# Converting float64 weights on chip: the high mantissa masked into 8 to 9, two additions to VectorE's share, GpSimd's share taken away

## The chip, the cores and the metric

The kernel runs on one core of a Trainium2 chip. The metric is the device time of one execution in microseconds (us). Of the kernel before there are three timed runs and one profiled execution, whose trace gives every instruction's start and duration.

## The reference

An mLSTM cell with 4 batches, 8 heads, 768 positions and 40 features per head is followed by a feed-forward block. Per head and position:

```
m_new  = max(f + m, i);  f_stab = exp(f + m - m_new);  i_stab = exp(i - m_new)
C = f_stab * C + i_stab * (v outer k);   n = f_stab * n + i_stab * k
y = sigmoid(o) * (C q) / max(|n . q|, 1)
x = y as (3072, 320)
h = x @ w_in          # (320, 2048)
out = (h - tanh(h)) @ w_out    # (2048, 320)
```

The two weight matrices arrive as float64. They are sent to the chip as 64-bit integers, and the kernel makes float32 of them.

## The kernel before

The sequence is cut into units of 128 positions of one batch, 24 in all. For each unit the cell part loads q, k, v, the output gate and a row `E` of gate products; VectorE scans `E` (line 363, 128x1024); TensorE makes the scores `ps`, which VectorE multiplies into `E` (line 394); TensorE makes `ph` from `E`, from the carried `state` and from `qg`, and `pc`, the new part of the state, which VectorE adds (lines 434 and 436); VectorE divides and gates (lines 416 to 421, the last writes `ys`), and TensorE transposes `ys` into `px`, which ScalarE copies to `xT`. GpSimd prepares `vs` (line 376), `qg` (line 379) and the decayed `state` (line 383) in `prepare`.

Two units make a group of 256 tokens. For a group and a pair of feature blocks, `up` makes `ph_up` from `xT` and `w_in` (12 matmuls as the profile counts them), ScalarE squares it twice (`z`, `q`, lines 500 and 501), VectorE makes `gt` of that (lines 502 and 503), and `down`, two items later, multiplies `gt` by `w_out` into `po`. Where the pairs of a group are done in more than one run, `po` is evicted into `part` (line 521 on VectorE, 523 on ScalarE); `po` has one buffer per token tile, so the next accumulation waits for the eviction.

The order on TensorE is written out by hand: `keep` chains every matmul to the one before. `STAGES` lists which pairs of which groups are taken in which order while the cell is still at work, and `merge` mixes the pieces of cell, feed-forward and conversion by their costs. On the other engines the framework's scheduler sets the order within what the data allow, and each engine then works through its own queue in that order.

The weights are 40 blocks: for each of the 8 pairs three of `w_in` (two of 128x256, one of 64x256) and two of `w_out` (128x320). A block is converted in three parts, a step apart from one another, so that the magnitude comes two steps after the fetch, and the sign two after that (`convert`, line 313; `weights`, line 273):

- fetch: the 64-bit words go to the staging tile `w64` (shown as `w`), eight buffers, from SP's queue (line 283);
- magnitude: VectorE masks the exponent out of the high word into `w_e` (295) and shifts the high word's mantissa up into `w_m` (298); ScalarE turns the exponent into the float's power of two (296), the shifted mantissa into a float of 1 to 2 (299) and the low word into a float `w_r` (300); GpSimd adds the two (301) and multiplies by the power of two (302);
- sign: VectorE takes the sign from the high word and sets it on `w_r` into `w_in` or `w_out` (306).

TensorE needs a pair's weights for the first time early in the cell part, so the conversion is spread over the same stretch as the cell and the first feed-forward items.

Of the kernel before, what the change touches and what calls it, by code (L numbers as in the profile page):

```python
# [34 lines left out]
FP = mybir.dt.float32  # L35
BF = mybir.dt.bfloat16
I32 = mybir.dt.int32
I64 = mybir.dt.int64
U32 = mybir.dt.uint32
AF = mybir.ActivationFunctionType  # L40
OP = mybir.AluOpType
# [20 lines left out]
def kernel(  # L62
# [14 lines left out]
    V, A, G = nc.vector, nc.scalar, nc.gpsimd  # L77
# [54 lines left out]
    conv = ctx.enter_context(tc.tile_pool(name="conv", bufs=2))  # L132
# [85 lines left out]
    for w in (after, ones):  # L218
        p = ps_b.tile([w.shape[1], NT, BH], FP, name="psum_lf", tag="b")
# [12 lines left out]
    xr, n, f = (mlp.tile([L, 2, NR], FP, name=name, tag=tag) for name, tag in (("xr", "z"), ("n", "z"), ("f", "q")))  # L232
# [40 lines left out]
    def weights(dst, src):  # L273

        p, n = dst.shape
        w = {}

        def fetch():
            if src.dtype == FP:
                nc.sync.dma_start(out=dst, in_=src)  # L280
                return
            w["st"] = conv.tile([128, n], I64, name="w64", tag="w64", bufs=8)[0:p]
            nc.sync.dma_start(out=w["st"], in_=src)

        def magnitude():
            if src.dtype == FP:
                return
            hi = w["hi"] = w["st"].bitcast(I32).rearrange("p (n two) -> p n two", two=2)[:, :, 1]
            lo = w["st"].bitcast(U32).rearrange("p (n two) -> p n two", two=2)[:, :, 0]
            e = conv.tile([128, n], I32, name="w_e", tag="w_e")[0:p]  # L290
            m = conv.tile([128, n], I32, name="w_m", tag="w_m")[0:p]
            r = w["r"] = conv.tile([128, n], I32, name="w_r", tag="w_r", bufs=4)[0:p]
            mf, rf = m.bitcast(FP), r.bitcast(FP)

            V.tensor_single_scalar(e, hi, 0x7FF00000, op=OP.bitwise_and)  # L295
            A.activation(out=e, in_=e, func=AF.Relu, scale=8.0, bias=rebias[0:p])  # L296

            V.tensor_single_scalar(m, hi, 12, op=OP.logical_shift_left)
            A.activation(out=mf, in_=m.bitcast(U32), func=AF.Copy, scale=2.0 ** -32, bias=1.0)  # L299
            A.activation(out=rf, in_=lo, func=AF.Copy, scale=2.0 ** -52)  # L300
            G.tensor_tensor(out=rf, in0=rf, in1=mf, op=OP.add)  # L301
            G.tensor_tensor(out=rf, in0=rf, in1=e.bitcast(FP), op=OP.mult)  # L302

        def sign():
            if src.dtype != FP:
                V.scalar_tensor_tensor(out=dst.bitcast(I32), in0=w["hi"], scalar=-(1 << 31), in1=w["r"],  # L306
                                       op0=OP.bitwise_and, op1=OP.bitwise_or)

        return fetch, magnitude, sign

    WB = 2 * 128

    def convert():

        blocks = []
        for p in range(NP):
            cols = slice(p * WB, (p + 1) * WB)
            for c, (r0, rows) in enumerate(KC):
                blocks.append(weights(w_in[0:rows, c, cols], moe_w_in[r0:r0 + rows, cols]))
            for f in (2 * p, 2 * p + 1):  # L320
                blocks.append(weights(w_out[:, f, :], moe_w_out[f * 128:(f + 1) * 128, :]))
        steps = []
        for x in range(len(blocks) + 4):
            def step(x=x):
                for late, part in enumerate((0, None, 1, None, 2)):
                    if part is not None and 0 <= x - late < len(blocks):
                        blocks[x - late][part]()
            steps.append((1.0, step))
        return steps
# [381 lines left out]
```

## Time and profile before

| | us |
|---|---|
| three runs, median (lowest, highest) | 682.23 (682.13, 682.42) |
| the profiled execution, whole | 682.25 |
| its span, first to last instruction | 680.5 |
| TensorE busy (matmul) | 612.6 |
| VectorE busy | 361.4 |
| ScalarE busy | 222.3 |
| GpSimd busy | 157.9 |

Engines are named PE (TensorE matmul), PEld (its weight load), DVE (VectorE), ACT (ScalarE), POOL (GpSimd) and SP (the queue that starts most transfers). A row of a group reads: line, engine, operation, out<-in, shape, count, then busy us and mean ns of one, then the engine's idle time just before these instructions and what ended most of it. A row of the timeline reads: start, duration, engine, line, operation, and in brackets the idle time before it and what ended it. Rows that follow one another closely are merged, with their count. The span between the starts of two successive operations can be shorter than a duration, since they overlap a little.

### The profile page before, as it was taken

The page shows a single profiled execution, that of the slowest core. Times are in us where ns is not written, and L with a number is a line of the kernel's source. Part 1 is how long each engine was busy: PE and PEld are TensorE (multiplying, and loading weights), DVE is VectorE, ACT ScalarE, POOL GpSimd, SP SyncE. Part 2 cuts the span into 40 slices and gives each one's busy share as a digit, 9 for nine tenths or more (in the row PEclk, how much of TensorE's full clock was granted, in tenths as well). Part 3 has the DMA queues.
Part 4 walks back from the last instruction along what each step waited for, and adds up shares of the span by engine and source line. Part 5 has one row for each costly group of instructions (what it writes and reads, how often), then busy time and mean ns, then how long its engine had stood idle before and what let it go on. Part 6 is the DMA issues. An engine that isn't in the chain of part 4 may idle for free.

```text
span 680.5 us, 8577 instructions
## 1 busy us (share of the span) xinstructions
PE 612.6 (90%) x3100; PEld 509.7 (75%) x3100; DVE 361.4 (53%) x617; ACT 222.3 (33%) x511; POOL 157.9 (23%) x170
## 2 busy tenths in 40 slices
PE   1469779787779999999999999999999999999996
PEld 1368657665667888888888888888888888878784
DVE  8686778977776336655553543553353333332321
ACT  2313545434632222322223322333233232242321
POOL 7534648645642010220220120111011000000000
PEclk9775979789979999999999999999999999999999
DMA  5637726346212011222221221221010000000000
GB/s 164 185 93 202 227 66 177 104 153 195 93 35 89 1 39 51 91 85 83 89 90 33 76 89 48 91 79 60 31 61 29 1 1 19 1 20 0 21 0 25
DMA packets 46210, 50.97 MB, mean 75 GB/s; under 512 B 3984, under 2 KB 38416, under 8 KB 46160
## 3 DMA queue, kind: packets, MB, share of 16 engines
q1 hardware_dynamic: 42288, 46.22, 22.5%
q10 hardware_dynamic: 3872, 4.13, 1.8%
q8 instruction: 26, 0.43, 0.2%
q14 instruction: 24, 0.20, 0.1%
HBM read 46.20 MB, written 4.13 MB: 74 GB/s over the span
## 4 chain that ended last, share of the span: by engine, by line
PE 78%; DVE 11%; issue 3%; POOL 3%; DMA 2%; ACT 2%; SPq 1%; ACTq 0%; DVEq 0%; POOLq 0%
PE ph_up L92 34%; PE po L92 28%; PE ps L92 6%; PE ph L92 6%; DVE E L363 2%; PE pc L92 2%; POOL w_r L301 2%; POOL w_r L302 1%; DMA E<-f_rows 1%; PE px L96 1%; DVE w_out L306 1%; DVE gt L503 1%; DVE gt L502 1%; DVE w_in L306 1%; DVE w_e L295 1%
## 5 line engine op out<-in xcount | busy, mean ns | idle before, releaser
L92 PE MATMUL ph_up<-xT,w_in 128*128 128x256 f32 x1152 | 318.9, 396 | 9.7 <-DVE gt L502 4.7
L92 PE MATMUL po<-w_out,gt 128*128 128x320 f32 x768 | 252.4, 442 | 3.9 <-DVE part L521 3.9
L92 PEld LDWEIGHTS ph_up<-xT,w_in 128*128 128x128 f32 x1152 | 203.1, 195 | 37.6 <-DVE gt L502 5.2
L502 DVE SCALAR_TENSOR_TENSOR gt<-ph_up,z 128x512 f32<-128x512 f32 x96 | 66.0, 689 | 208.5 <-ACT z L500 208.4
L92 PEld LDWEIGHTS po<-w_out,gt 128*128 128x128 f32 x768 | 132.7, 192 | 33.2 <-DVE part L521 4.9
L500 ACT ACTIVATE z<-ph_up 128x512 f32<-128x512 f32 x96 | 57.2, 595 | 253.7 <-PE ph_up L92 253.6
L92 PEld LDWEIGHTS ps<-q,kz 128*128 128x128 f32 x384 | 74.6, 218 | 21.2 <-DVE E L394 8.9
L92 PE MATMUL ps<-q,kz 128*128 128x128 f32 x384 | 80.2, 308 | 8.6 <-DVE E L394 8.6
L92 PEld LDWEIGHTS ph<-vs,E 128*128 128x128 f32 x384 | 71.7, 208 | 10.2 <-issue 0.5
L503 DVE SCALAR_TENSOR_TENSOR gt<-q,gt 128x512 f32<-128x512 f32 x96 | 70.6, 736 | 7.5 <-ACT q L501 1.4
L501 ACT ACTIVATE q<-z,tiny 128x512 f32<-128x512 f32 x96 | 69.1, 721 | 2.8
L92 PE MATMUL ph<-vs,E 128*128 128x41 f32 x384 | 61.9, 260 | 0.0
L363 DVE TENSOR_TENSOR_SCAN E<-E,diag 128x1024 f32<-128x1024 f32 x24 | 56.0, 2338 | 10.2 <-DMA E<-f_rows 10.2
L376 POOL TENSOR_TENSOR vs<-v,ei 128x640 f32<-128x640 f32 (+1 forms) x24 | 28.5, 1188 | 127.6 <-PE ph L92 123.0
L383 POOL TENSOR_TENSOR state<-state,eT 80x328 f32<-80x328 f32 x16 | 11.7, 734 | 163.7 <-DVE state L434 117.2
L394 DVE TENSOR_TENSOR E<-ps,E 128x512 f32<-128x512 f32 x48 | 32.9, 687 | 29.4 <-PE ps L92 29.0
L301 POOL TENSOR_TENSOR w_r<-w_r,w_m 128x256 f32<-128x256 f32 (+2 forms) x40 | 33.3, 834 | 58.6 <-ACT w_m L299 45.5
L92 PEld LDWEIGHTS pc<-vs,k 128*80 128x80 f32 x160 | 23.1, 170 | 21.8 <-issue 11.3
L379 POOL TENSOR_TENSOR qg<-qg,q 80x512 f32<-80x512 f32 x20 | 35.9, 1794 | 10.0 <-DMA qg<-g_rows 6.1
L92 PEld LDWEIGHTS ph<-state,qg 128*128 128x128 f32 x160 | 30.5, 197 | 9.7 <-issue 1.1
L92 PE MATMUL pc<-vs,k 128*80 128x82 f32 x160 | 25.3, 260 | 13.4 <-DVE ys L421 7.9
L296 ACT ACTIVATE w_e<-w_e,rebias 128x256 int32<-128x256 int32 (+2 forms) x40 | 21.0, 525 | 45.2 <-DVE w_e L295 45.1
(89 smaller groups left out, 368.9 us busy)
## 6 DMA issues: line engine op xcount, KB each, us to landing
E<-f_rows SPq DMA_DIRECT2D x24, 512.0 KB
w<-in_moe_w_out SPq DMA_DIRECT2D x16, 320.0 KB
w<-in_moe_w_in SPq DMA_DIRECT2D x16, 256.0 KB
kz<-in_kT SPq DMA_DIRECT2D x48, 80.0 KB
q<-in_qT SPq DMA_DIRECT2D x48, 80.0 KB
v<-in_v SPq DMA_DIRECT2D x24, 160.0 KB
k<-in_k SPq DMA_DIRECT2D x24, 160.0 KB
o<-in_o_gate SPq DMA_DIRECT2D x24, 160.0 KB
```

The costliest lines, as they stand in the source:

```text
L92: return cls.keep(nc.tensor.matmul(*args, **kwargs))
L296: A.activation(out=e, in_=e, func=AF.Relu, scale=8.0, bias=rebias[0:p])
L301: G.tensor_tensor(out=rf, in0=rf, in1=mf, op=OP.add)
L306: V.scalar_tensor_tensor(out=dst.bitcast(I32), in0=w["hi"], scalar=-(1 << 31), in1=w["r"], op0=OP.bitwise_and, op1=OP.bitwise_or)
L363: V.tensor_tensor_scan(out=row, data0=row, data1=diag.rearrange("p h t -> p (h t)"), initial=0.0, op0=OP.mult, op1=OP.add)
L376: G.tensor_tensor(out=t["vs"][:, both, :, 0:D], in0=t["v"].unsqueeze(1).to_broadcast(shape), in1=scale.unsqueeze(3).to_broadcast(shape), o ...
L379: G.tensor_tensor(out=t["qg"][0:TOP], in0=t["qg"][0:TOP], in1=t["q2"][0:TOP], op=OP.mult)
L394: V.tensor_tensor(out=P, in0=t["ps"], in1=P, op=OP.mult)
L500: A.activation(out=z, in_=ph, func=AF.Square, accum_out=sums[:, g * NP + p:g * NP + p + 1])
L501: A.activation(out=q, in_=z, func=AF.Square, bias=tiny)
L502: V.scalar_tensor_tensor(out=gt, in0=ph, scalar=TINY_POLY[0], in1=z, op0=OP.mult, op1=OP.mult)
L503: V.scalar_tensor_tensor(out=gt, in0=q, scalar=TINY_POLY[2], in1=gt, op0=OP.add, op1=OP.mult)
```

## The change

The magnitude's part is replaced by `split`, the sign's by `join`; the staging, the blocks and their steps stay.

- In `split` the two masks on VectorE stay, but the second now keeps the high word's 20 mantissa bits and sets the bits of 8.0 above them in the same instruction, which gives a float between 8 and 9. ScalarE makes the power of two and the low word's float as before; its conversion of the mantissa is gone.
- In `join` VectorE subtracts 7 and adds the low word's float, sets the sign on the power of two, and multiplies the two into the weight tile.
- GpSimd has no part in it any more.
- `w_e`, `w_m` and `w_r` have three buffers each; before, these were two, two and four.

```diff
-        def magnitude():
+        def split():
...
-            e = conv.tile([128, n], I32, name="w_e", tag="w_e")[0:p]
-            m = conv.tile([128, n], I32, name="w_m", tag="w_m")[0:p]
-            r = w["r"] = conv.tile([128, n], I32, name="w_r", tag="w_r", bufs=4)[0:p]
-            mf, rf = m.bitcast(FP), r.bitcast(FP)
+            e, m, r = (conv.tile([128, n], I32, name=name, tag=name, bufs=3)[0:p] for name in ("w_e", "w_m", "w_r"))
+            w["e"], w["m"], w["r"] = e, m, r
...
-            V.tensor_single_scalar(m, hi, 12, op=OP.logical_shift_left)
-            A.activation(out=mf, in_=m.bitcast(U32), func=AF.Copy, scale=2.0 ** -32, bias=1.0)
-            A.activation(out=rf, in_=lo, func=AF.Copy, scale=2.0 ** -52)
-            G.tensor_tensor(out=rf, in0=rf, in1=mf, op=OP.add)
-            G.tensor_tensor(out=rf, in0=rf, in1=e.bitcast(FP), op=OP.mult)
-
-        def sign():
-            if src.dtype != FP:
-                V.scalar_tensor_tensor(out=dst.bitcast(I32), in0=w["hi"], scalar=-(1 << 31), in1=w["r"],
-                                       op0=OP.bitwise_and, op1=OP.bitwise_or)
+            V.tensor_scalar(out=m, in0=hi, scalar1=0xFFFFF, scalar2=0x41000000, op0=OP.bitwise_and, op1=OP.bitwise_or)
+            A.activation(out=r.bitcast(FP), in_=lo, func=AF.Copy, scale=2.0 ** -52)
+
+        def join():
...
+            V.scalar_tensor_tensor(out=r, in0=m, scalar=-7.0, in1=r, op0=OP.add, op1=OP.add)
+            V.scalar_tensor_tensor(out=e, in0=w["hi"], scalar=-(1 << 31), in1=e, op0=OP.bitwise_and, op1=OP.bitwise_or)
+            V.tensor_tensor(out=dst, in0=r, in1=e.bitcast(FP), op=OP.mult)
```

One line fewer stands above them, so that after the change lines behind the conversion have a number lower by one (363 becomes 362, 502 becomes 501, 521 becomes 520); the masks are lines 293 and 296 now, the joining operations 304 to 306. The order on TensorE is the same, and GpSimd's is the same without its rows on `w_r`. VectorE's and ScalarE's orders are mixed anew.

The first place is VectorE's queue at the first eviction into `part` (tiles 208 and 209; the numbers behind `w_` are those of the staging tiles). Before, from the scan of `E` on:

```order
L363 SCALAR_TENSOR_TENSOR E<-E,diag 128x1024
L502 SCALAR_TENSOR_TENSOR gt<-ph_up,z 128x512
L503 SCALAR_TENSOR_TENSOR gt<-q,gt 128x512
L295 TENSOR_SCALAR w_e<-w_659 64x256
L298 TENSOR_SCALAR w_m<-w_659 64x256
L521 TENSOR_TENSOR part_208<-po,part_208 128x320
L521 TENSOR_TENSOR part_209<-po,part_209 128x320
```

Now, with 21 rows of conversion and one of `gt` between the same scan and the first of these:

```order
L293 TENSOR_SCALAR w_e<-w_743 64x256
L305 SCALAR_TENSOR_TENSOR w_e<-w_707,w_e 128x256
L501 SCALAR_TENSOR_TENSOR gt<-ph_up,z 128x512
L306 TENSOR_TENSOR w_in<-w_r,w_e 128x256
L502 SCALAR_TENSOR_TENSOR gt<-q,gt 128x512
L293 TENSOR_SCALAR w_e<-w_767 128x320
L296 TENSOR_SCALAR w_m<-w_767 128x320
L304 SCALAR_TENSOR_TENSOR w_r<-w_m,w_r 128x256
L305 SCALAR_TENSOR_TENSOR w_e<-w_721,w_e 128x256
L520 TENSOR_TENSOR part_208<-po,part_208 128x320
L306 TENSOR_TENSOR w_in<-w_r,w_e 128x256
L520 TENSOR_TENSOR part_209<-po,part_209 128x320
```

The eviction stood directly behind `gt` and two masks; now 28 rows of conversion in all, of seven blocks, lie between the scan and it.

The second place is VectorE's queue one scan earlier, at the gating of a unit (`ys_220`). Before:

```order
L306 SCALAR_TENSOR_TENSOR w_out<-w_500,w_r 128x320
L417 TENSOR_TENSOR den<-den,ph 128x8
L418 RECIPROCAL den<-den 128x8
L419 TENSOR_TENSOR o<-o,den 128x320
L421 TENSOR_TENSOR ys_220<-ph,o 128x320
L363 SCALAR_TENSOR_TENSOR E<-E,diag 128x1024
```

Now:

```order
L306 TENSOR_TENSOR w_in<-w_r,w_e 64x256
L416 TENSOR_TENSOR den<-den,ph 128x8
L304 SCALAR_TENSOR_TENSOR w_r<-w_m,w_r 128x320
L417 RECIPROCAL den<-den 128x8
L362 SCALAR_TENSOR_TENSOR E<-E,diag 128x1024
L418 TENSOR_TENSOR o<-o,den 128x320
L305 SCALAR_TENSOR_TENSOR w_e<-w_490,w_e 128x320
L420 TENSOR_TENSOR ys_220<-ph,o 128x320
```

The scan stood behind `ys`; now it stands ahead of the last two gating steps, with parts of a block's conversion between them.

More of the change, by code (lines that the diff above doesn't have):

```diff
@@ L289, in magnitude @@
             lo = w["st"].bitcast(U32).rearrange("p (n two) -> p n two", two=2)[:, :, 0]
-            e = conv.tile([128, n], I32, name="w_e", tag="w_e")[0:p]
-            m = conv.tile([128, n], I32, name="w_m", tag="w_m")[0:p]
-            r = w["r"] = conv.tile([128, n], I32, name="w_r", tag="w_r", bufs=4)[0:p]
-            mf, rf = m.bitcast(FP), r.bitcast(FP)
+            e, m, r = (conv.tile([128, n], I32, name=name, tag=name, bufs=3)[0:p] for name in ("w_e", "w_m", "w_r"))
+            w["e"], w["m"], w["r"] = e, m, r
             V.tensor_single_scalar(e, hi, 0x7FF00000, op=OP.bitwise_and)
             A.activation(out=e, in_=e, func=AF.Relu, scale=8.0, bias=rebias[0:p])
-            V.tensor_single_scalar(m, hi, 12, op=OP.logical_shift_left)
-            A.activation(out=mf, in_=m.bitcast(U32), func=AF.Copy, scale=2.0 ** -32, bias=1.0)
-            A.activation(out=rf, in_=lo, func=AF.Copy, scale=2.0 ** -52)
-            G.tensor_tensor(out=rf, in0=rf, in1=mf, op=OP.add)
-            G.tensor_tensor(out=rf, in0=rf, in1=e.bitcast(FP), op=OP.mult)
-        def sign():
-            if src.dtype != FP:
-                V.scalar_tensor_tensor(out=dst.bitcast(I32), in0=w["hi"], scalar=-(1 << 31), in1=w["r"],
-                                       op0=OP.bitwise_and, op1=OP.bitwise_or)
-        return fetch, magnitude, sign
+            V.tensor_scalar(out=m, in0=hi, scalar1=0xFFFFF, scalar2=0x41000000, op0=OP.bitwise_and, op1=OP.bitwise_or)
+            A.activation(out=r.bitcast(FP), in_=lo, func=AF.Copy, scale=2.0 ** -52)
+        def join():
+            if src.dtype == FP:
+                return
+            e, m, r = w["e"], w["m"].bitcast(FP), w["r"].bitcast(FP)
+            V.scalar_tensor_tensor(out=r, in0=m, scalar=-7.0, in1=r, op0=OP.add, op1=OP.add)
+            V.scalar_tensor_tensor(out=e, in0=w["hi"], scalar=-(1 << 31), in1=e, op0=OP.bitwise_and, op1=OP.bitwise_or)
+            V.tensor_tensor(out=dst, in0=r, in1=e.bitcast(FP), op=OP.mult)
+        return fetch, split, join
     WB = 2 * 128
```

## The prediction

> **What bounds the kernel now.** I read the page's slices first. TensorE (PE) fills the last three quarters, at full clock; the first 12 of 40 slices, about 200 us, are broken up, VectorE (DVE) is busiest there and GpSimd (POOL) works almost only there.
>
> ```profile
> span 680.5 us, 8577 instructions
> PE   1469779787779999999999999999999999999996
> DVE  8686778977776336655553543553353333332321
> POOL 7534648645642010220220120111011000000000
> PEclk9775979789979999999999999999999999999999
> ```
>
> The busy time by stretches (columns: PE, weight load, DVE, ACT, POOL, granted clock, DMA share, GB/s) says what that is worth. From 164 to 198 us VectorE works a little longer than PE. From 212 us on PE works 462.06 of 468.5 us, so nothing can be won or lost there, and whatever the front gives moves the end by as much.
>
> ```profile
> 164.00:198.00 34.00, 25.63 (x129) 21.28 (x130) 26.36 (x50) 16.73 (x42) 18.83 (x22) 0.85 0.19 57
> 212.00:680.50 468.50, 462.06 (x2327) 380.57 (x2325) 197.03 (x320) 136.24 (x299) 38.62 (x32) 1.00 0.14 45
> ```
>
> The groups by line, for 17 to 212 us alone, show PE idle for VectorE: 4.7 for `gt`, 3.2 for `w_in`, 3.9 for `part`, 7.9 for `ys`, 8.3 for `state`, and 5.5 whose release the profile does not name, 33.5 us together.
>
> ```profile
> L92 PE MATMUL ph_up<-xT,w_in 128*128 128x256 f32 x192 | 59.1, 432 | 9.7 <-DVE gt L502 4.7 <-DVE w_in L306 3.2 <-ACT xT L445 1.1
> L92 PE MATMUL po<-w_out,gt 128*128 128x320 f32 x109 | 36.6, 454 | 3.9 <-DVE part L521 3.9
> L92 PE MATMUL pc<-vs,k 128*80 128x82 f32 x72 | 12.0, 290 | 13.4 <-DVE ys L421 7.9 <-issue 5.5
> L96 PE MATMUL px<-ident,ys 128*128 128x128 f32 x24 | 5.6, 336 | 9.4 <-DVE state L434 8.3 <-ACT q L501 1.0
> ```
>
> So VectorE is the late engine, and the same view shows what holds it: the conversion's own four groups wait 9.5 + 4.8 + 4.5 + 5.1 = 23.9 us for GpSimd's two steps on `w_r`, and their mean durations are far above their best.
>
> ```profile
> L306 DVE SCALAR_TENSOR_TENSOR w_in<-w,w_r 128x256 int32<-128x256 int32 (+1 forms) x24 | 20.2, 847 | 9.5 <-POOL w_r L302 9.5
> L295 DVE TENSOR_SCALAR w_e<-w 128x256 int32<-128x256 int32 (+2 forms) x40 | 18.1, 453 | 4.8 <-POOL w_r L302 4.8
> L298 DVE TENSOR_SCALAR w_m<-w 128x256 int32<-128x256 int32 (+2 forms) x40 | 17.2, 432 | 4.5 <-POOL w_r L301 4.5
> L503 DVE SCALAR_TENSOR_TENSOR gt<-q,gt 128x512 f32<-128x512 f32 x15 | 13.3, 889 | 0.9 <-ACT q L501 0.4
> L306 DVE SCALAR_TENSOR_TENSOR w_out<-w,w_r 128x320 int32<-128x320 int32 x16 | 13.2, 824 | 5.1 <-POOL w_r L302 5.1
> L502 DVE SCALAR_TENSOR_TENSOR gt<-ph_up,z 128x512 f32<-128x512 f32 x15 | 10.1, 681 | 6.3 <-ACT z L500 6.3
> ```
>
> The timeline of VectorE says why the means are high. The same form at line 306 takes 0.41 us (128x256) or 0.48 us (128x320) and lets the next start after 0.33 or 0.41 us when GpSimd rests, but one took 3.78 us.
>
> ```profile
> 20.97 0.28 DVE L295 TENSOR_SCALAR w_e<-w 128x256 int32<-128x256 int32 x1
> 37.27 0.31 DVE L298 TENSOR_SCALAR w_m<-w 128x320 int32<-128x320 int32 x1
> 39.47 3.78 DVE L306 SCALAR_TENSOR_TENSOR w_in<-w,w_r 64x256 int32<-64x256 int32 x1 [0.61 <-POOL w_r L302]
> 59.72 0.41 DVE L306 SCALAR_TENSOR_TENSOR w_in<-w,w_r 128x256 int32<-128x256 int32 x1
> 60.05 0.16 DVE L417 TENSOR_TENSOR den<-den,ph 128x8 f32<-128x8 f32 x1
> 92.42 0.69 DVE L502 SCALAR_TENSOR_TENSOR gt<-ph_up,z 128x512 f32<-128x512 f32 x1 [1.87 <-ACT z L500]
> 93.22 0.69 DVE L503 SCALAR_TENSOR_TENSOR gt<-q,gt 128x512 f32<-128x512 f32 x1
> 102.29 0.48 DVE L306 SCALAR_TENSOR_TENSOR w_out<-w,w_r 128x320 int32<-128x320 int32 x1
> 102.70 0.81 DVE L298 TENSOR_SCALAR w_m<-w 64x256 int32<-64x256 int32 x1
> ```
>
> GpSimd's timeline has the reason: four operations stood back to back from 39.39 until 42.96, and the one at 39.47 ended 0.29 us behind the last.
>
> ```profile
> 39.39 0.73 POOL L383 TENSOR_TENSOR state<-state,eT 80x328 f32<-80x328 f32 x1
> 40.08 0.85 POOL L301 TENSOR_TENSOR w_r<-w_r,w_m 128x320 f32<-128x320 f32 x1
> 40.90 1.26 POOL L376 TENSOR_TENSOR vs<-v,ei 128x640 f32<-128x640 f32 x1
> 42.11 0.85 POOL L302 TENSOR_TENSOR w_r<-w_r,w_e 128x320 f32<-128x320 f32 x1
> ```
>
> I read this as VectorE operations whose operands all lie in SBUF not running while GpSimd works. The `gt` step that reads PSUM is not held: L502 has a mean of 681 ns in the groups above, L503, all in SBUF, 889, and undisturbed both take 0.69.
>
> **The change part by part.** *GpSimd's two steps go.* It did 80 of them; VectorE's 23.9 us of idle for them goes with them, and so do blocked starts. Those were, mean less best: 24 x (0.847 - 0.41) = 10.5, 16 x (0.824 - 0.48) = 5.5, 40 x (0.453 - 0.30) = 6.1, 40 x (0.432 - 0.30) = 5.3, and for L503 15 x (0.889 - 0.69) = 3.0, in all 30.4 us. Not all of it is the conversion's doing: `vs`, `state` and `qg` stay on GpSimd, three for each of some nine units in the front, 0.73 (`state`) to 1.26 us (`vs`) in the rows above, about 27 us. With two more conversion operations open to them I let them block 11 us still (a start falls into one with about the share of time that VectorE spends on such operations, and then waits half of it; bounds 0 and 27). So 30.4 - 11 = 19.4 goes.
>
> *VectorE gets two more operations per block*: both are of line 306's kind, two inputs in SBUF. 24 blocks x 2 x 0.33 + 16 x 2 x 0.41 = 15.8 + 13.1 = 28.9 us. One of them (sign onto the power) is word for word the old form on another tile; the add and the product are floats, for which the nearest row is L503 (0.69 for 512 columns, scaling to about the same 0.33 for 256). The mask now carries two operations in one instruction. No undisturbed row shows that pair; between no extra and the two-input price it costs 0 to 24 x 0.13 + 16 x 0.17 = 5.8; I take 0, since it reads one tile like L298, and keep 5.8 for the range.
>
> *ScalarE loses one of three conversions per block*, 40 in all. It was late only because its inputs were, so I count 0. The low word's operation now may have to wait for a buffer (three instead of four), freed by the product three blocks earlier; behind it in ScalarE's queue stand `z` and `q`, for which `gt` waits. Those blocks are several VectorE operations apart in the new order, so 0, at worst some 0.3 us in each of 40.
>
> *The order on VectorE moves*, at the two places shown with the change. The eviction of `part` now stands behind a lump of conversions.
>
> ```profile
> 88.27 2.28 DVE L363 TENSOR_TENSOR_SCAN E<-E,diag 128x1024 f32<-128x1024 f32 x1
> 94.23 0.87 DVE L521 TENSOR_TENSOR part<-po,part 128x320 f32<-128x320 f32 x2
> 102.66 1.24 PE L92 MATMUL po<-w_out,gt 128*128 128x320 f32 x4
> ```
>
> Before, it began 5.96 us behind the scan's start; now a scan, three `gt` steps, 14 masks and 14 joining operations (8 and 6 of the two widths) come first: 2.28 + 3 x 0.69 + 14 x 0.21 + 8 x 0.33 + 6 x 0.41 = 12.4 us. PE came to the product that needs it at 102.66, 7.6 us behind its end at 95.10; 6.4 of these are used up, and what PE gains ahead of this place beyond the rest becomes a wait. In another unit `ys` comes behind the scan, 2.3 us later. I charge 4 us for both (bounds 0 and 6.4 + 2.3 = 8.7). SP's queue waits for the staging tile until the sign has been read, as before, one operation earlier now; 0.
>
> *Sum on VectorE*: -23.9 - 19.4 + 28.9 = -14.4 us in the front. PE adds the cost of its stalls: after a long wait its clock is low for a while. Twelve equal matmuls took 5.01 us behind the stall of 4.74, and 2.75 shortly behind one of 2.29.
>
> ```profile
> 86.60 5.01 PE L92 MATMUL ph_up<-xT,w_in 128*128 128x256 f32 x12 [4.74 <-DVE gt L502]
> 123.86 0.53 PE L92 MATMUL pc<-vs,k 128*80 128x82 f32 x2 [5.30 <-DVE ys L421]
> 164.04 2.42 PE L92 MATMUL po<-w_out,gt 128*128 128x320 f32 x8 [2.29 <-DVE part L521]
> 166.29 2.75 PE L92 MATMUL ph_up<-xT,w_in 128*128 128x256 f32 x12
> 191.12 0.66 PE L96 MATMUL px<-ident,ys 128*128 128x128 f32 x2 [8.33 <-DVE state L434]
> ```
>
> Three stalls of the long kind stand here; if they shrink to about 2 us, the clock gives 3 x 2.3 = 6.9 more (bounds 0 and that). I take it whole, since a VectorE operation held up stands ahead of each. Together -14.4 - 6.9 + 4 = -17.3. What is late next is PE's own work; the most there is to win from its waits is the 33.5 us.
>
> *A rule against the change.* Both added two-input forms read two float or integer tiles, 32 bits wide. The Trainium skill, Vector Engine (DVE) Microarchitecture Reference, Points that are easy to get wrong, states that a scalar-tensor-tensor operation with two SBUF inputs that are not bf16 runs at half throughput. The trace does not agree: L503 (both in SBUF) and L502 (one in PSUM) stand at 0.69 us above.
>
> **The rivals.** *PE takes over (all stalls go).* GpSimd's share of the blocked starts goes too: the 33.5 us of PE's stalls shrink by four fifths, 27, and 6 of slow clock with them: 682.25 - 33 = 649. For it: each of the stalls has a blocked VectorE operation ahead of it. Against: VectorE's lane by itself gives 14. Chance 0.15.
>
> *The new order eats it.* Eviction and `ys` behind the lumps cost their full 8.7, and the clock gives nothing: -14.4 + 8.7 = -5.7, 677. For it: the two places are certain, the order shows them. Against: only one unit is so in each. Chance 0.20, of which 0.03 end within 0.2%.
>
> *Slower: VectorE as the longer queue.* The 28.9 us all stand on the path, since VectorE is the late engine, while only what the chain of waits shows of GpSimd goes, 3% of the span or 20.4 us; the blocked starts were then time in which PE would have waited anyhow or pass to `vs`, `qg` and `state`. +28.9 - 20.4 = +8.5: 691. It decides once less than about 5 us of the blocked starts comes back. For it: a second input in SBUF is just what GpSimd holds up, and 80 more such operations stand open to it. Against: the 3.78 us row, where two of the four holders were the conversion's own. Chance 0.16.
>
> ```profile
> PE 78%; DVE 11%; issue 3%; POOL 3%; DMA 2%; ACT 2%; SPq 1%; ACTq 0%; DVEq 0%; POOLq 0%
> ```
>
> *Half-rate adds.* If the float add with two 32-bit SBUF inputs ran at half rate, it would take 0.27 us (128x256) or 0.33 us (128x320) more: 24 x 0.27 + 16 x 0.33 = 11.8, so -17.3 + 11.8 = -5.5: 677. By the rows of L502 and L503, 0.04, a quarter of it within 0.2%. This is the mechanism of the rule above.
>
> **How the numbers follow.** The profiled execution took 682.25 us (span 680.5), the median of the three runs shown is 682.23. Forecast 682.25 - 17.3 = 665, chance 0.45 (658 to 671). PE taking over, 649, has 0.15; the order's 677 0.20; VectorE's queue, 691, 0.16; the half rate's 677 0.04. About 0.2%, 1.4 us, is what a measurement of this kernel can tell. Faster: 0.45 + 0.15 + 0.17 + 0.03 = 0.80; the same: 0.03 + 0.01 = 0.04; slower 0.16. The range from 650 to 681 leaves out most of the slower case and the lower half of the best one; it holds the two-operation mask at 5.8.
>
> **What would show it.** In the profile after: no `w_r` on GpSimd, and VectorE's idle for it gone; the masks' means near 0.30 and the three joining operations near 0.41 and 0.48; PE's `state` and `ys` stalls shorter, a `part` stall near 95 us that was not there. Wrong it is if the joining operations stand at 0.6 or more, if PE idles more than 33.5 us in the front for VectorE, or if E's or the weights' transfers end PE's waits.

## The result and the profile after

The changed kernel took 655.65 us (median of four runs, 653.40 to 656.31) against 682.18 for the kernel before, now the median of four. The ratio is 0.961, with a 95% interval of 0.958 to 0.964: 26.5 us faster, where 17.3 were forecast. The direction and the range (650 to 681) were right. The size was too small by 9 us: the time lies below the 658 to 671 of the forecast's own case, and nearer to the 649 of the rival in which PE takes over than to the forecast's 665.

The page's slices of the kernel after: TensorE (PE) is nearly full from the seventh slice on, where before it was broken up until the twelfth, and GpSimd (POOL) has thinned out.

```profile
span 654.1 us, 8562 instructions
...
PE   1376879999899999999999999999999999999994
DVE  8797999999962356556436436435433332322231
POOL 7412303310220102202202201101101000000000
PEclk9878888999999999999999999999999999999999
```

The same by stretches, first the front of the kernel before, then the front and the rest of the kernel after (length, busy us of PE, weight load, VectorE, ScalarE and GpSimd, granted clock, DMA share, GB/s):

```profile
17.00:212.00 195.00, 147.49 (x759) 126.80 (x760) 150.00 (x268) 81.89 (x206) 106.30 (x117) 0.83 0.47 140
```

```profile
17.00:186.00 169.00, 138.26 (x768) 118.68 (x769) 158.88 (x350) 71.55 (x167) 41.31 (x37) 0.91 0.54 163
186.00:654.10 468.10, 459.91 (x2318) 378.90 (x2316) 194.62 (x319) 135.40 (x297) 36.17 (x32) 1.00 0.14 44
```

The front ends at 186 instead of 212 us with about the same matmuls done (759 and 768 by the records); the rest takes 468.1 us as against 468.5. So all of the gain lies in the front, 26 us. It can be counted on either engine. On VectorE busy time rose by 8.9 us and idle time fell from 45.0 to 10.1, by 34.9: together -26.0. The same front counted on PE: busy time fell by 9.2 (the granted clock rose from 0.83 to 0.91) and idle time from 47.5 to 30.7, by 16.8: -26.0 again, as it must be, since both are the front's length. After the change VectorE is busy for 158.88 of 169 us.

VectorE's groups of the conversion and of `gt` after, for the front alone: no idle time in front of any of them, where 23.9 us for GpSimd and 6.3 for `z` stood before.

```profile
L305 DVE SCALAR_TENSOR_TENSOR w_e<-w,w_e 128x256 int32<-128x256 int32 (+2 forms) x40 | 22.4, 560 | 0.0
L304 DVE SCALAR_TENSOR_TENSOR w_r<-w_m,w_r 128x256 f32<-128x256 f32 (+2 forms) x40 | 19.2, 479 | 0.0
L293 DVE TENSOR_SCALAR w_e<-w 128x256 int32<-128x256 int32 (+2 forms) x40 | 16.2, 404 | 0.0
L296 DVE TENSOR_SCALAR w_m<-w 128x256 int32<-128x256 int32 (+2 forms) x40 | 15.1, 378 | 0.0
L501 DVE SCALAR_TENSOR_TENSOR gt<-ph_up,z 128x512 f32<-128x512 f32 x16 | 10.8, 678 | 0.0
L502 DVE SCALAR_TENSOR_TENSOR gt<-q,gt 128x512 f32<-128x512 f32 x15 | 10.2, 683 | 0.0
L306 DVE TENSOR_TENSOR w_in<-w_r,w_e 128x256 f32<-128x256 f32 (+1 forms) x24 | 10.0, 416 | 0.0
L306 DVE TENSOR_TENSOR w_out<-w_r,w_e 128x320 f32<-128x320 f32 x16 | 8.4, 523 | 0.0
```

PE's groups in the front: its waits for VectorE are 0.9 for `w_in`, 4.0 for `part`, 4.0 and 2.9 ahead of `pc`, 2.7 + 1.0 + 0.9 ahead of `px`, 16.4 us in all instead of 33.5 (the waits for `E` and `f`, 8.6 and 5.3 us before and 8.7 and 5.3 after, are left out of both). One `ph_up` takes 403 ns on the mean instead of 432.

```profile
L92 PE MATMUL ph_up<-xT,w_in 128*128 128x256 f32 x198 | 55.6, 403 | 2.6 <-ACT xT L444 1.1 <-DVE w_in L306 0.9 <-DMA w<-in_moe_w_in 0.6
L92 PE MATMUL po<-w_out,gt 128*128 128x320 f32 x112 | 38.1, 461 | 4.0 <-DVE part L520 4.0
L92 PE MATMUL pc<-vs,k 128*80 128x82 f32 x72 | 10.9, 268 | 7.0 <-DVE ys L420 4.0 <-issue 2.9
L96 PE MATMUL px<-ident,ys 128*128 128x128 f32 x24 | 4.4, 279 | 4.7 <-DVE ys L420 2.7 <-DVE state L433 1.0 <-DVE state L435 0.9
```

PE's timeline shows the two new waits that the prediction had placed, for the `ys` behind the scan and for `part` near 95 us; the four `po` behind the second took 2.50 us, about twice what they take undisturbed (1.24 in an experiment below).

```profile
73.27 0.52 PE L96 MATMUL px<-ident,ys 128*128 128x128 f32 x3 [2.74 <-DVE ys L420]
...
96.52 2.50 PE L92 MATMUL po<-w_out,gt 128*128 128x320 f32 x4 [3.84 <-DVE part L520]
```

### The profile page after: what moved, and what is told of

Its sections match the earlier page's. It is cut to its first block, busy times and chain, and to the rows that moved or that the text cites. A ratio compares the mean times of both kernels' runs of the same rounds, so it can differ in the third digit from the quotient of the medians.

```text
span 654.1 us, 8562 instructions
## 1 busy us (share of the span) xinstructions
PE 601.2 (92%) x3100; PEld 499.9 (76%) x3100; DVE 367.9 (56%) x697; ACT 211.1 (32%) x471; POOL 90.4 (14%) x90
## 4 chain that ended last, share of the span: by engine, by line
PE 80%; DVE 11%; DMA 3%; issue 3%; SPq 1%; POOL 1%; ACT 0%; ACTq 0%; DVEq 0%; POOLq 0%
PE ph_up L92 35%; PE po L92 30%; PE ph L92 6%; PE ps L92 5%; PE pc L92 2%; DMA E<-f_rows 2%; DVE E L362 2%; DVE w_e L305 1%; PE px L96 1%; DVE w_m L296 1%; DVE w_e L293 1%; DVE w_r L304 1%; DVE gt L501 1%; SPq L161 1%; DVE E L393 1%
## 5 line engine op out<-in xcount | busy, mean ns | idle before, releaser
L92 PE MATMUL ph_up<-xT,w_in 128*128 128x256 f32 x1152 | 314.0, 392 | 2.6 <-ACT xT L444 1.1
L92 PEld LDWEIGHTS ph_up<-xT,w_in 128*128 128x128 f32 x1152 | 200.5, 192 | 29.9 <-ACT xT L444 2.4
L92 PEld LDWEIGHTS ps<-q,kz 128*128 128x128 f32 x384 | 70.7, 207 | 20.4 <-DVE E L393 9.0
L92 PE MATMUL ps<-q,kz 128*128 128x128 f32 x384 | 76.6, 297 | 8.7 <-DVE E L393 8.7
L92 PEld LDWEIGHTS ph<-vs,E 128*128 128x128 f32 x384 | 69.5, 201 | 10.7 <-issue 0.8
L502 DVE SCALAR_TENSOR_TENSOR gt<-q,gt 128x512 f32<-128x512 f32 x96 | 67.6, 705 | 6.6 <-ACT q L500 1.0
L362 DVE TENSOR_TENSOR_SCAN E<-E,diag 128x1024 f32<-128x1024 f32 x24 | 54.7, 2283 | 12.1 <-DMA E<-f_rows 12.1
L375 POOL TENSOR_TENSOR vs<-v,ei 128x640 f32<-128x640 f32 (+1 forms) x24 | 31.0, 1295 | 151.1 <-PE ph L92 128.0
L378 POOL TENSOR_TENSOR qg<-qg,q 80x512 f32<-80x512 f32 x20 | 31.6, 1582 | 42.2 <-DMA qg<-g_rows 38.5
L92 PE MATMUL ph<-state,qg 128*128 128x82 f32 x160 | 28.1, 258 | 1.5 <-issue 1.5
L297 ACT ACTIVATE w_r<-w 128x256 f32<-128x256 uint32 (+2 forms) x40 | 18.3, 460 | 32.3 <-DVE w_in L306 16.6
```

Of the source, the lines that this page charges most:

```text
L92: return cls.keep(nc.tensor.matmul(*args, **kwargs))
L297: A.activation(out=r.bitcast(FP), in_=lo, func=AF.Copy, scale=2.0 ** -52)
L362: V.tensor_tensor_scan(out=row, data0=row, data1=diag.rearrange("p h t -> p (h t)"), initial=0.0, op0=OP.mult, op1=OP.add)
L375: G.tensor_tensor(out=t["vs"][:, both, :, 0:D], in0=t["v"].unsqueeze(1).to_broadcast(shape), in1=scale.unsqueeze(3).to_broadcast(shape), o ...
L378: G.tensor_tensor(out=t["qg"][0:TOP], in0=t["qg"][0:TOP], in1=t["q2"][0:TOP], op=OP.mult)
L502: V.scalar_tensor_tensor(out=gt, in0=q, scalar=TINY_POLY[2], in1=gt, op0=OP.add, op1=OP.mult)
```

## The experiments

The theory: GpSimd's work on SBUF by itself holds VectorE up, beside the waits for its results, and VectorE is late in the front, so what it loses or wins comes out in the time. The rivals: only the waits for `w_r` counted; ScalarE's saved step did it; the new order on VectorE did it; or PE has become the bound, so that VectorE's time is worth little. The ratios are to the kernel before, run on the same chip in each set.

### GpSimd's work alone: two and one idle products per block

`zeros` is a tile of zeros, set once.

```diff
             A.activation(out=r.bitcast(FP), in_=lo, func=AF.Copy, scale=2.0 ** -52)
+            x = conv.tile([128, n], FP, name="w_x", tag="w_x", bufs=2)[0:p]
+            for _ in range(2):                       # pool_idle_one: range(1)
+                G.tensor_tensor(out=x, in0=hi.bitcast(FP), in1=zeros[0:p, 0:n], op=OP.mult)
```

> The changed kernel, with two more GpSimd products per block (80 in all) that read the high word of the staging tile and a tile of zeros and write a scratch tile that nobody reads; no engine waits for their result, only the staging tile's next transfer comes behind them. Theory (GpSimd holds VectorE up by being at work): the conversion's means, 0.40 and 0.38 us for the masks and 0.48 and 0.56 for the first two joining operations, go back to those of before or above, some 0.1 to 0.3 us over five operations in 40 blocks, 20 us or more; VectorE is busy 158.9 of 169 us in the front, so most of it comes out: 665 to 680 us. Rival (what went were waits for GpSimd's results alone, the blocked starts cost nothing): 656 us within 2.

> The changed kernel with one idle GpSimd product per block instead of two, some 50 us of GpSimd's time. Theory (the cost goes with the time that GpSimd works): half of the 35 us that two cost, 670 to 676. Rival (GpSimd's work costs only where it keeps vs, qg or state waiting, as bursts of 15 products did): 656 to 662, like the 40 memsets' 660.

Measured: 690.56 us with two (ratio 1.015, 1.010 to 1.020), 675.24 with one (0.990, 0.987 to 0.994). With two the kernel is slower than the one before, though no engine needs any of these results. GpSimd's group of them, for 17 to 215 us, with two and then with one:

```profile
L303 POOL TENSOR_TENSOR w_x<-w,zeros 128x256 f32<-128x256 f32 (+2 forms) x80 | 102.9, 1299 | 21.6 <-DMA w<-in_moe_w_in 14.1 <-DMA w<-in_moe_w_out 4.7
```

```profile
L303 POOL TENSOR_TENSOR w_x<-w,zeros 128x256 f32<-128x256 f32 (+2 forms) x40 | 55.6, 1411 | 29.4 <-DMA w<-in_moe_w_in 23.3 <-DMA w<-in_moe_w_out 6.2
```

VectorE's groups of the kernel with two, for 17 to 186 us (the lines stand 3 to 6 higher): the masks are at 502 and 496 ns instead of 404 and 378, the first two joining operations at 647 and 644 instead of 479 and 560, with no idle time in front of them to speak of. They are held, they do not wait for a semaphore.

```profile
L310 DVE SCALAR_TENSOR_TENSOR w_r<-w_m,w_r 128x256 f32<-128x256 f32 (+2 forms) x34 | 22.0, 647 | 0.0
L311 DVE SCALAR_TENSOR_TENSOR w_e<-w,w_e 128x256 int32<-128x256 int32 (+2 forms) x34 | 21.9, 644 | 0.0
L296 DVE TENSOR_SCALAR w_e<-w 128x256 int32<-128x256 int32 (+2 forms) x36 | 18.1, 502 | 0.0
L299 DVE TENSOR_SCALAR w_m<-w 128x256 int32<-128x256 int32 (+2 forms) x36 | 17.8, 496 | 0.8 <-DMA w<-in_moe_w_in 0.8
```

By the traces, VectorE, ScalarE, TensorE and SP's queue do the same operations in the same order as in the changed kernel, with two products and with one. For the 350 operations that VectorE did in the 169 us of the changed kernel's front it needs, with two:

```profile
17.00:217.20 200.20, 149.57 (x769) 126.91 (x770) 195.24 (x350) 71.69 (x167) 141.86 (x118) 0.86 0.47 138
```

VectorE is busy for 195.24 us instead of 158.88, and idle for 5.0, of which 0.8 ended on a transfer into a staging tile. What follows: neither the waits alone, nor the order, nor a staging tile that comes free later can be the cause. The cost goes with GpSimd's time: 19.6 us for 55.6, 34.9 for 102.9, 0.35 and 0.34 us for each. Two was dearer than expected (665 to 680), since an idle product took 1.30 us and not the 0.85 of the old steps. Not all of it is VectorE's: PE also waited directly for these products (shown as `w_x`, 1.9 us with two, 1.4 with one), as they stand ahead of `vs`, `qg` and `state` in GpSimd's queue.

### GpSimd emptied

```diff
-        G.tensor_tensor(out=t["vs"][:, both, :, 0:D], ...
+        V.tensor_tensor(out=t["vs"][:, both, :, 0:D], ...
-            G.tensor_tensor(out=t["qg"][0:TOP], ...
+            V.tensor_tensor(out=t["qg"][0:TOP], ...
-                G.tensor_tensor(out=new, in0=old, ...
+                V.tensor_tensor(out=new, in0=old, ...
```

> The changed kernel with vs, qg and state on VectorE too, so that GpSimd does nothing after its memsets. In the front 12 products of about 0.83 us, 8 of 0.69 and 9 of 0.45 by the shapes, 19.5 us more on VectorE, and no operation is held up any more: means less best over masks, joining operations and scan, 14.6 us, go. Theory (GpSimd's work costs VectorE about its own time): 655 to 663, near to even. Rival (VectorE's queue pays the whole 19.5 and wins nothing back, since the blocked starts cost nothing): 668 to 675.

Measured: 660.65 us (0.969, 0.966 to 0.973), inside the theory's range. VectorE's groups for 17 to 186 us: both masks stand at 288 and 289 ns, the joining operations at 437 and 434. Nothing holds them any more.

```profile
L304 DVE SCALAR_TENSOR_TENSOR w_r<-w_m,w_r 128x256 f32<-128x256 f32 (+2 forms) x35 | 15.3, 437 | 1.5 <-ACT w_r L297 1.5
L305 DVE SCALAR_TENSOR_TENSOR w_e<-w,w_e 128x256 int32<-128x256 int32 (+2 forms) x35 | 15.2, 434 | 0.3 <-ACT w_e L294 0.3
L293 DVE TENSOR_SCALAR w_e<-w 128x256 int32<-128x256 int32 (+2 forms) x38 | 10.9, 288 | 0.0
L296 DVE TENSOR_SCALAR w_m<-w 128x256 int32<-128x256 int32 (+2 forms) x37 | 10.7, 289 | 0.0
```

So the excess that was left in the changed kernel came from `vs`, `qg` and `state`. By the shapes 19.5 us of work went to VectorE and the kernel lost 5, so most of it was paid back. The stretch in which TensorE does the same 768 matmuls as in the changed kernel's front:

```profile
17.00:191.00 174.00, 144.56 (x768) 125.56 (x769) 154.54 (x363) 70.10 (x165) 2.40 (x8) 0.95 0.54 158
```

VectorE is not busier in it than before (154.5 and 158.9 us, with three or four blocks of the conversion still to be joined), but idle for 19.5 us instead of 10.1: the loss shows as waiting. The scheduler mixed VectorE's order anew here, and how much of the 5 us that makes no run shows. Going all the way is no gain here.

### VectorE's own work: one operation more, one less

```diff
             V.tensor_tensor(out=dst, in0=r, in1=e.bitcast(FP), op=OP.mult)
+            V.tensor_tensor(out=x, in0=r, in1=e.bitcast(FP), op=OP.mult)      # vec_more, x a scratch tile
```

```diff
-            V.scalar_tensor_tensor(out=r, in0=m, scalar=-7.0, in1=r, op0=OP.add, op1=OP.add)
...
-            V.tensor_tensor(out=dst, in0=r, in1=e.bitcast(FP), op=OP.mult)
+            V.scalar_tensor_tensor(out=dst, in0=m, scalar=-7.0, in1=e.bitcast(FP), op0=OP.add, op1=OP.mult)   # vec_less
```

> The changed kernel, with one more VectorE product per block into a scratch tile that nobody reads: 24 x 0.33 + 16 x 0.41 = 14.5 us more on VectorE. Theory (VectorE's queue is what bounds the front, busy 158.9 of 169 us there): 12 to 17 us slower than the changed kernel, 668 to 673. Rival (after the change TensorE bounds the front, whose waits for VectorE are only some 16 us in a few places): a third or less of it, 657 to 661.

> The changed kernel without the low word's addition: VectorE's first joining operation goes and the product takes the mask's value less 7 directly, so 14.5 us of VectorE's work go; the low word, the weights' last bits, is left out (ScalarE still makes its float, which nobody reads). Theory (VectorE's queue bounds the front): 8 to 15 us faster than the changed kernel, 641 to 648, less than the whole since TensorE's waits for VectorE are only some 16 us. Rival (TensorE bounds the front): 653 to 656.

Measured: 666.69 us with one more (0.978, 0.975 to 0.981), 652.90 with one less (0.958, 0.955 to 0.962). Eleven of 14.5 us come out on the one side, which is between the two expectations and nearer the theory's; on the other side 2.8 at most, and by the intervals perhaps nothing. The theory fell there. In the kernel with one less VectorE has 23.6 us idle of 169 (windows), and its groups for 17 to 186 us say what it waits for now: `E`'s transfer and ScalarE's `z`, which comes from PE's product.

```profile
17.00:186.00 169.00, 142.40 (x775) 122.58 (x776) 145.44 (x312) 69.59 (x167) 42.54 (x37) 0.89 0.56 163
```

```profile
L361 DVE TENSOR_TENSOR_SCAN E<-E,diag 128x1024 f32<-128x1024 f32 x13 | 31.1, 2395 | 6.5 <-DMA E<-f_rows 6.5
...
L500 DVE SCALAR_TENSOR_TENSOR gt<-ph_up,z 128x512 f32<-128x512 f32 x16 | 10.8, 678 | 6.4 <-ACT z L498 6.4
```

The changed kernel therefore stands near a corner: more work on VectorE costs three quarters of itself, less of it wins next to nothing. Both prices hold the order as well as the work, since the scheduler mixed VectorE's order anew in both kernels, and `gate_first` below shows that another order alone can cost 9 us.

### ScalarE's third conversion put back

```diff
-            V.tensor_scalar(out=m, in0=hi, scalar1=0xFFFFF, scalar2=0x41000000, op0=OP.bitwise_and, op1=OP.bitwise_or)
+            V.tensor_single_scalar(m, hi, 12, op=OP.logical_shift_left)
+            A.activation(out=m.bitcast(FP), in_=m.bitcast(U32), func=AF.Copy, scale=2.0 ** -32, bias=1.0)
...
-            V.scalar_tensor_tensor(out=r, in0=m, scalar=-7.0, in1=r, op0=OP.add, op1=OP.add)
+            V.tensor_tensor(out=r, in0=m, in1=r, op=OP.add)
```

> The changed kernel with the old way to the mantissa: VectorE shifts it up, ScalarE turns it into a float (40 more operations of 0.43 us, 17.1 us), VectorE adds and does not subtract 7. GpSimd stays out. Theory (the gain is from GpSimd's absence): ScalarE is busy 71.6 of 169 us in the front and the join comes two steps later, so 656 us within 2. Rival (the saved step on ScalarE is a good part of the gain): 17 us on the way to the join, 665 to 673.

Measured: 654.40 us (0.960, 0.957 to 0.963), the same as the changed kernel. The mask into 8 to 9 and the saved step on ScalarE gave nothing here; the gain lies in where the additions and products are done.

### Half of it back to GpSimd

```diff
-            V.tensor_tensor(out=dst, in0=r, in1=e.bitcast(FP), op=OP.mult)
+            G.tensor_tensor(out=dst, in0=r, in1=e.bitcast(FP), op=OP.mult)
```

> The changed kernel with the last product of each block on GpSimd: VectorE has 14.5 us less, GpSimd 40 operations of some 0.85 us more, and TensorE waits for GpSimd's product. Theory (GpSimd's work holds VectorE up): VectorE's masks and joining operations go up by 0.1 to 0.2 us again, the 80 idle operations cost 35 us, so 40 cost half of that, 17, against at most 3 us that the kernel with one VectorE operation less won: 665 to 673. Rival (sharing the work relieves VectorE): 645 to 653.

Measured: 661.43 us (0.971, 0.968 to 0.975): slower than the changed kernel, so sharing does not relieve, but by 5.8 us, less than expected. GpSimd's groups of these products in the front:

```profile
L306 POOL TENSOR_TENSOR w_in<-w_r,w_e 128x256 f32<-128x256 f32 (+1 forms) x24 | 28.2, 1177 | 36.9 <-DVE w_e L305 35.6 <-DVE w_r L304 1.3
L306 POOL TENSOR_TENSOR w_out<-w_r,w_e 128x320 f32<-128x320 f32 x16 | 17.2, 1073 | 22.2 <-DVE w_e L305 21.8 <-DVE den L416 0.4
```

For 45.4 us of GpSimd's time the idle products would give some 16 us. The masks and joining operations did not rise by 0.1 to 0.2 us as the theory had it: for 17 to 186 us they stand at 382, 341, 479 and 545 ns, beside 404, 378, 479 and 560 in the changed kernel. The scan (2573 instead of 2278), line 502 (800 instead of 683) and line 418 (894 instead of 490) rose. To the same 768 matmuls:

```profile
17.00:193.70 176.70, 145.49 (x768) 124.45 (x769) 152.77 (x309) 69.99 (x167) 83.73 (x77) 0.87 0.52 156
```

VectorE's busy time fell by 6.1 us and not by the 14.5 that were taken from it, and its idle time rose from 10.1 to 23.9. Of the idle time 5.0 us ended on GpSimd's products, as did 4.1 us of PE's waits. So the loss shows as waiting, for GpSimd's products among others; VectorE's order is mixed anew here too, and no run parts the two.

### A GpSimd operation that reads nothing

```diff
+            x = conv.tile([128, 1024], FP, name="w_x", tag="w_x", bufs=1)
+            G.memset(x, 0.0)
```

> The changed kernel with one GpSimd memset of a scratch tile of 128x1024 per block, 40 of about 1.05 us by the 0.79 of the one of 128x768, which nobody reads or waits for: 42 us more of GpSimd's work that reads nothing. Theory (any work of GpSimd on SBUF holds VectorE): some 42/103 of the 35 us that 103 us of idle products cost, 668 to 674. Rival (only GpSimd's operations with tensor inputs hold it): VectorE's masks and joining operations keep their means, 655 to 659.

Measured: 660.08 us (0.970, 0.968 to 0.973): 4.4 us slower than the changed kernel, between the two. VectorE's groups for 17 to 186 us explain it (lines two higher behind the split): the masks rose from 404 and 378 to 513 and 479 ns, the joining operations did not rise, 458 and 529 against 479 and 560.

```profile
L307 DVE SCALAR_TENSOR_TENSOR w_e<-w,w_e 128x256 int32<-128x256 int32 (+2 forms) x40 | 21.2, 529 | 0.0
L293 DVE TENSOR_SCALAR w_e<-w 128x256 int32<-128x256 int32 (+2 forms) x40 | 20.5, 513 | 0.0
L296 DVE TENSOR_SCALAR w_m<-w 128x256 int32<-128x256 int32 (+2 forms) x40 | 19.2, 479 | 0.4 <-DMA w<-in_moe_w_in 0.4
L306 DVE SCALAR_TENSOR_TENSOR w_r<-w_m,w_r 128x256 f32<-128x256 f32 (+2 forms) x40 | 18.3, 458 | 0.0
```

The two timelines of this kernel show it case by case, GpSimd's and then VectorE's. Six memsets run from 41.31 to 47.30, and the joining operations and the scan inside them take their usual time; the masks at 49.05, 60.28 and 61.38 take 1.04 to 1.11 us, with memsets at work. Line 504, a `gt` step with two inputs in SBUF, did rise, to 816 ns, by two operations of 1.74 and 1.76 us; these two ran beside `vs` and `qg`, and so did every joining operation of lines 306 and 307 over 0.52 us run beside `vs`, `qg` or `state`. The order of VectorE is that of the changed kernel.

```profile
41.31 5.99 POOL L299 MEMSET w_x<- 128x1024 f32 x6
...
47.94 3.09 POOL L299 MEMSET w_x<- 128x1024 f32 x3
...
59.26 5.09 POOL L299 MEMSET w_x<- 128x1024 f32 x5
```

```profile
42.71 0.47 DVE L306 SCALAR_TENSOR_TENSOR w_r<-w_m,w_r 128x320 f32<-128x320 f32 x1
43.11 0.47 DVE L307 SCALAR_TENSOR_TENSOR w_e<-w,w_e 128x320 int32<-128x320 int32 x1
...
44.30 2.29 DVE L364 TENSOR_TENSOR_SCAN E<-E,diag 128x1024 f32<-128x1024 f32 x1 [0.19 <-DMA E<-f_rows]
...
49.05 1.08 DVE L296 TENSOR_SCALAR w_m<-w 128x320 int32<-128x320 int32 x1
...
60.28 1.11 DVE L296 TENSOR_SCALAR w_m<-w 128x256 int32<-128x256 int32 x1
...
61.38 1.04 DVE L293 TENSOR_SCALAR w_e<-w 64x256 int32<-64x256 int32 x1
```

So neither expectation holds as put: a write-only operation of GpSimd holds the one-input masks and lets two-input operations pass; one with tensor inputs holds both.

### The order on VectorE

```diff
+                    with tc.high_priority():
-                    V.tensor_tensor(out=part[n], in0=po[tt], in1=part[n], op=OP.add)
+                        V.tensor_tensor(out=part[n], in0=po[tt], in1=part[n], op=OP.add)
```

That is `part_first`. `gate_first` puts the six steps of `gate` that end in `ys` under the same line as well, and `before_gate_first` makes both edits to the kernel before.

> The changed kernel, with the eviction of part and the six steps that end in ys put ahead in the scheduler's order, so that on VectorE they no longer stand behind masks, joining operations or the scan; the operations are the same. Theory (after the change TensorE's remaining waits for part, 4.0, and ys, 6.7 us, are the price of the new order, as the prediction charged): 5 to 10 us faster than the changed kernel, 646 to 651. Rival (VectorE is busy 158.9 of 169 us in the front, so the waits only pass to the weights or gt): 653 to 657.

> The changed kernel with the eviction of part alone put ahead in the scheduler's order; on VectorE it then stands some 20 rows earlier at the first place, and later rows shift too. Theory (each place's wait is the price of what stands ahead of it, the prediction's 6.4 us for this place): the wait of 3.84 us for part goes and a microsecond of slow clock with it, 650 to 653. Rival (VectorE is full, the wait passes to the conversion or gating behind it, as it did when ys was put ahead as well, 664.9): 654 to 662.

> The kernel before, with the same steps put ahead in the scheduler's order and nothing else changed. Theory (GpSimd's work and the waits for it cost the time of before): TensorE's waits for ys (7.9) and part (3.9) shrink at most, 674 to 683 us. Rival (the order on VectorE, which the change mixed anew, brought the gain, not GpSimd's absence): 656 to 668.

Measured: `before_gate_first` 681.40 us (1.000, 0.998 to 1.002), so an order of this kind alone brings nothing. Nor does the changed kernel's own order: `pool_idle` has it and loses the whole gain. (GpSimd's order is not quite that of before either: by the traces a few of `vs`, `qg` and `state` changed places.) `part_first` 655.97 (0.962, 0.961 to 0.964), no change from the changed kernel; `gate_first` 664.89 (0.977, 0.975 to 0.979), 9 us slower, which neither side expected. In `part_first` the wait for `part` is gone (the product there starts at 94.23 with no wait), and PE stands for 4.57 us ahead of 110.30, with no releaser named, where the changed kernel has no wait:

```profile
94.23 1.24 PE L92 MATMUL po<-w_out,gt 128*128 128x320 f32 x4
...
110.30 0.69 PE L92 MATMUL ph<-state,qg 128*128 128x82 f32 x2 [4.57 <-issue]
```

In `gate_first` the same place costs 5.07 us. The timeline of all engines there shows on VectorE a mask that waited 1.74 us for its staging tile and was then held for 2.18 by `qg` and `vs`, and behind it the steps up to `ys`, which ended at 111.58; PE went on at 111.80. `ys` is the last reader of the `ph` whose buffer the next product takes.

```profile
105.74 2.18 DVE L296 TENSOR_SCALAR w_m<-w 128x256 int32<-128x256 int32 x1 [1.74 <-DMA w<-in_moe_w_in]
...
111.10 0.48 DVE L421 TENSOR_TENSOR ys<-ph,o 128x320 f32<-128x320 f32 x1
...
111.80 0.69 PE L92 MATMUL ph<-state,qg 128*128 128x82 f32 x2 [5.07 <-issue]
```

To the same 768 matmuls VectorE in `gate_first` is busy for 159.0 us, as in the changed kernel, and idle for 19.6 instead of 10.1, so that the loss is all waiting. Why it loses 9 us in all stays open: the order of SP's transfers changed along with VectorE's, and no run parts the two.

### A fourth buffer

```diff
-            e, m, r = (conv.tile([128, n], I32, name=name, tag=name, bufs=3)[0:p] for name in ("w_e", "w_m", "w_r"))
+            e, m, r = (conv.tile([128, n], I32, name=name, tag=name, bufs=4)[0:p] for name in ("w_e", "w_m", "w_r"))
```

> The changed kernel with four buffers instead of three for each of the conversion's tiles. Theory (ScalarE's waits for a buffer of w_r, 27.6 us, lie beside other work, as the prediction put them at 0): 655 within 2. Rival (they delay z, q and with them gt, and cost TensorE its waits for gt and the weights): 648 to 652.

Measured: 654.37 us (0.960, 0.958 to 0.962), the same as with three. ScalarE's wait for a buffer of `w_r`, 27.6 us with three and 12.9 with four, costs nothing, as the prediction had it. No version tried beats the changed kernel by more than the intervals tell, the one without the low word included.

## Why the prediction was right, and where its size came from

**GpSimd's hold on VectorE: right, and shown.** The idle products price it with the order unchanged, the emptied GpSimd takes it away. The prediction's form of it, for every operation whose operands all lie in SBUF, is too wide: memsets held the masks alone. The forecast let 30.4 us of blocked starts shrink to 11; by the groups after, means less best (0.30 for the masks, 0.438 on the mean for lines 304 and 305, 0.41 and 0.48 for 306), it is 40 x 0.104 + 40 x 0.078 + 40 x 0.041 + 40 x 0.122 + 24 x 0.006 + 16 x 0.043 = 4.2 + 3.1 + 1.6 + 4.9 + 0.1 + 0.7 = 14.6. So 15.8 went, not 19.4. The forecast had put the time of `vs`, `qg` and `state` at about 27 us; GpSimd's groups have 39.9 of them in the front before (`qg` alone 17.8, 2.23 each) and 39.7 after.

**The signs.** GpSimd's `w_r` and VectorE's idle time for it are gone, PE's waits for `state` and `ys` shrank from 8.3 and 7.9 to 1.9 and 6.7 us, and the `part` stall came. The masks at 404 and 378 ns and line 305 at 560 missed the 0.30 and the 0.41 to 0.48 us that were to be seen.

**VectorE's added work: right as durations.** Lines 304 and 305 stand at 437 and 434 ns in the emptied kernel, which is the mean of 0.41 and 0.48 us over 24 and 16 blocks; the two-operation mask stands at 289 beside 288 for the other one. Blocked starts and added work together were to make VectorE busier by 28.9 - 19.4 = 9.5 us; the windows show 8.9.

**The step that failed is the sum on VectorE.** It put VectorE's idle time down by 23.9 us, the part that ended on GpSimd, took the other 21.1 us as fixed, and so charged the 28.9 us of added work whole. The windows show -34.9 us of idle time. The missing 11.0 are waits for other engines: by the groups before and after, that for ScalarE's `z` went from 6.3 us to 0.0, those for PE's `ps` and `pc` from 4.1 and 4.1 to 1.6 and 1.4, while the wait for `E`'s transfer rose from 3.5 to 5.8. `vec_less` speaks for added work that fell into these waits: GpSimd is out of the conversion there too, VectorE has 14.5 us less to do, and it is idle for 23.6 us, near the 21.1, with 6.4 for `z` again. By these two kernels the last 14.5 us of added work cost 2.8. That it was the work and not the order mixed anew with it no run shows. -34.9 + 8.9 = -26.0 is the front's gain.

**The clock and the order were charged on top.** Both lie inside the same 26 us. The front's length is VectorE's busy and idle time, so a faster PE shows there as a shorter wait. PE's busy time did fall by 9.2 us with the clock, more than the 6.9 forecast, but this is PE's way of counting, beside an idle time down by 16.8. In a sum that left VectorE's other waits out, the 6.9 stood in for a part of the missing 11.0. The order's waits appeared exactly where forecast (2.74 and 3.84 us; the eviction began 12.1 us behind the scan's start, 12.4 were forecast), yet they are no price: in `part_first`, without the second, the time is the same and another place has a wait of 4.57 us. The errors add up: -11.0 for the idle time, -0.6 for the busy time, +2.9 for leaving out -6.9 + 4: -8.7, and -17.3 - 8.7 = -26.0.

**ScalarE at 0: right**, from both sides (`act_three`, `bufs4`).

**The rivals.** "PE takes over", 649, lies nearer to the measured time than the forecast does, and after the change relief for VectorE is worth 2.8 us of 14.5; but PE's waits for VectorE are halved, not down to a fifth. "Slower, VectorE as the longer queue" was to decide if less than 5 us of blocked starts came back; 15.8 did. It was not baseless: added work on VectorE does come out, 11 of 14.5 us in `vec_more`. "The new order eats it" (677) fell with the time itself. "Half-rate adds" fell with the rows of line 304: with GpSimd emptied, this float operation with two SBUF inputs takes 411 ns for 128x256 and 476 for 128x320, the plain product of line 306 takes 411 and 477. The rule that the prediction cited from the Trainium skill (Vector Engine (DVE) Microarchitecture Reference, Points that are easy to get wrong) would have it at half throughput; the trace does not agree, since it is no slower than the plain product.

## What to carry to other kernels

Work on GpSimd is not free where VectorE is the late engine: here each us of products cost 0.34 us of the kernel even when nobody needed the result, and each us of memsets 0.11 (4.4 for 38.8). So price a move off GpSimd by the waits and by the hold-ups that go, not by the operations added alone. Do not take the late engine's remaining idle time as fixed: here 11 us of it went as well, and added work can fall into it. Count such a gain on one engine from end to end, idle time for every releaser included; terms read off another engine (its clock, its waits) are the same time counted again. In a queue that is nearly full, a wait at one place was not the price of that place.

## What the runs showed of the hardware

A memset of GpSimd holds VectorE's one-input masks (means up by 0.11 and 0.10 us) and not its two-input operations (0.47 us inside a run of memsets), while products with tensor inputs hold both. This is how the Trainium skill puts it in SBUF — State Buffer, Who interferes with whom: an instruction of VectorE with two SBUF inputs contends with a GpSimd instruction that reads SBUF and not with one that only writes, and one in a two-port mode contends with GpSimd without that distinction. The trace agrees on both; that the masks run in such a mode no run shows directly.

A held operation shows no idle time ahead of it but a longer duration: line 306's form before, 0.41 us undisturbed, took 3.78 with four GpSimd operations back to back. The two-operation mask takes as long as the one-operation mask (289 and 288 ns with GpSimd emptied).
